# An adaLN block on one core: the second pair's second norm turned by DMA transposes, its first block two blocks later, and POOL or DVE chosen by a changed rule

## The chip, the cores and the metric

The kernel runs on one core of a Trainium2 chip. The metric is the device time of one execution in microseconds. The core's engines work side by side: TensorE (PE) multiplies matrices into PSUM, VectorE (DVE), ScalarE (ACT) and GpSimd (POOL) work on rows, and SyncE (SP) issues the DMAs. Each engine takes its own instructions strictly in the order in which the program gave them to it.

## The reference

A transformer block with adaptive layer norm; x has 2048 rows of 512 values, all in float32.

```python
mod = (_silu(c) @ w_mod).reshape(c.shape[0], 6, 1, -1)      # sa, ca, ga, sb, cb, gb
h = _layernorm(x) * (1 + ca) + sa
x = x + ga * attention(h)      # 32 heads of 128, the last 512 keys and values of the cache, @ wq, @ wo
h = _layernorm(x) * (1 + cb) + sb
x = x + gb * ((gelu(h @ w_gate) * (h @ w_up)) @ w_down)     # inner width 1376
```

## The kernel before

Every matrix product is taken from float16 halves: an operand is a high part and a low part (value minus high part), and a product is three matmuls, high by high, high by low and low by high. The making of these halves is much of what ACT, DVE and POOL do: a scaling of the raw weight, an ACT copy to float16, and a subtraction.

**Attention.** The rows are four groups of 512 (`qg`), two of which make a pair `p`. A slot takes one head and one group, 128 slots in all. It multiplies q by k into `psS` (a pair of PSUM banks, two of them in use), takes the row maxima on DVE (`st<-psS`, two per slot), the exponentials on ACT (`p`, `pp`), the low parts on POOL (`pp<-p,pp`, 128x1024), turns them by DMA transposes (`pT<-pp`), multiplies by v into `psO`, splits the result (`oT`), multiplies by wo into `psW`, and adds into `acc` on DVE. From the third pair of heads on, the q projection of a pair of groups and a pair of heads uses Winograd's form of Strassen's scheme, seven products in place of eight; its sums of weights and activations (`a_sum`, `t_full`, `t_sum`) are elementwise work too.

**The weights' crossings.** `spread_max` (line 667) gets four maxima to all partitions by way of DRAM, reduces them on DVE, turns them into scales `iv` by one tiny `tensor_scalar` on DVE, and takes the reciprocal `av`.

**The second norm and the feed-forward.** `ln_stats` makes mean and reciprocal deviation, `ln2_norm` (line 1363) the normed rows in float32, and `ln2_chunk` (line 1369) turns one of four column chunks by four PE transposes of 128x128 float32 into `psQ`, then applies scale and shift from PSUM. `ln2_high` and `ln2_low` split it. Pair 0 is groups 0 and 1; pair 1, the second pair, groups 2 and 3, made by `chunk2` (line 1817) from the steps in `P1` (line 1843). The inner width is cut into 11 blocks `f` of 128 (the last of 96). A unit `(p, f)` in `UNITS` (line 1764) is one block of one pair; with the same scheme its gate and up products are seven products of six matmuls, 42 matmuls. `aw_make` (line 1822) makes a unit's split weights and their sums; the units left out of `SPLIT` use those that the first pair made for the same block, which in this kernel are blocks 6 to 9 of the second pair.

**What sets the order.** Nothing is issued where the code stands. Every call on an engine is recorded by the `Weaver` with its reads and writes; `issue` (line 412) then plays the whole list several times with a table of costs, forwards and backwards and with random shifts, keeps the order that fares best by that table, and emits it. Some operations are recorded with `either`: the play gives them to one of two engines. `tt` (line 963) does so for POOL and DVE, and carries most subtractions and sums; `affine`, the norms and the scalings do so for other pairs of engines. For operations that hold a resource which POOL and DVE share in the play (the flag `lock`), `sooner` (line 273) adds `SHY`, 1500 ns, to DVE's end when it compares the two. Where POOL's operation is planned close behind such a DVE operation, `issue` makes POOL wait for it. So a change of any step, unit or rule gives a new order on all engines.

Of the kernel before, what the change touches and what calls it, by code (L numbers as in the profile page):

```python
# [10 lines left out]
F32 = mybir.dt.float32  # L11
F16 = mybir.dt.float16
BF16 = mybir.dt.bfloat16
AF = mybir.ActivationFunctionType
OP = mybir.AluOpType
# [3 lines left out]
P = 128  # L19
N = 512  # L20
# [9 lines left out]
NF = (DFF + P - 1) // P  # L30
# [8 lines left out]
HS = 2.0 ** 9  # L39
# [6 lines left out]
ROUND = 1.0 + 2.0 ** -7  # L46
# [43 lines left out]
class Weaver:  # L90
# [159 lines left out]
    def play(self, at, users, span, keep, cut):  # L250
# [6 lines left out]
        free, landed, bus, shared, order = {e: 0.0 for e in self.NEXT}, [], 0.0, {e: 0.0 for e in self.NEXT}, []  # L257
# [15 lines left out]
        def sooner(n, e, t):  # L273

            kinds = self.ops[n][4]
            mine = max(t, shared[e] if kinds[e][1] else 0.0) + kinds[e][0] + (e == "DVE" and kinds[e][1]) * self.SHY
            for o, kind in kinds.items():
                s = max(free[o], ready[n], shared[o] if kind[1] else 0.0)
                if o != e and s + kind[0] + (o == "DVE" and kind[1]) * self.SHY < mine:
                    return max(s, t) + 1.0  # L280
            return None

# [15 lines left out]
        while len(order) < len(self.ops):  # L298
            t, e = min((max(free[e], 0.0 if can[e] else wait[e][0][0]), e) for e in free if can[e] or wait[e])
            while wait[e] and wait[e][0][0] <= t:  # L300
                n = heapq.heappop(wait[e])[1]
# [3 lines left out]
            while can[e] and pick is None:  # L305
                x = heapq.heappop(can[e])
                n = x[1]
# [9 lines left out]
                if e != "SP":  # L317
                    s = pressing(n, e, t, t + self.ops[n][4][e][0] - self.NEXT[e] - 100.0)
# [4 lines left out]
                if len(self.ops[n][4]) > 1:  # L323
                    s = sooner(n, e, t)
# [11 lines left out]
            n = pick  # L336
            by[n] = e
            order.append(n)
            d, lock = self.ops[n][4][e][:2]
# [6 lines left out]
            if lock:  # L346
                t = max(t, shared[e])
# [6 lines left out]
            if e == "SP":  # L354
                if len(landed) >= self.LANES:
                    t = max(t, landed[-self.LANES])
# [95 lines left out]
def adaln_block(ctx: ExitStack, tc: tile.TileContext, x, k_cache, v_cache, wq, wo,  # L452
                w_gate, w_up, w_down, c_in, w_mod, out):
    nc = Weaver(tc.nc, tc)
# [15 lines left out]
    def small(pool, cols_, bufs=3, name="sm"):  # L470
        return pool.tile([P, cols_], F32, name=name, tag=name, bufs=bufs)
# [8 lines left out]
    acc = [rows_[:, t, :] for t in range(SQ // P)]  # L480
    cols = base.tile([P, 16], F32, name="cols")
    colA = {1: cols[:, 0:4], 2: cols[:, 8:12]}
    colB = {1: cols[:, 4:8], 2: cols[:, 12:16]}
# [11 lines left out]
    ffs = base.tile([P, 16], F32, name="ffs")  # L495
# [7 lines left out]
    def b_tile(p, nm, shape=(P, 2, 2, N), dtype=F16):  # L503
        return left1.tile(list(shape), dtype, name=f"{nm}_{p}", tag=f"{nm}_{p}", bufs=1)
# [30 lines left out]

    MV, RS, NMR, LNP, LNF = {}, {}, {}, {}, {}

    def ln_stats(key, src, j):
        if j == 0:
            MV[key] = base.tile([P, 4, 2], F32, name="mv", tag="mv", bufs=4)  # L540
            RS[key] = small(base, 4, 4, "rs")
        st = small(base, 6, 2, "bnst")
        nc.vector.bn_stats(st, src)
        nc.vector.bn_aggr(MV[key][:, j, :], st)
        if j == 3:
            ve = small(base, NC, 2, "ve")
            nc.gpsimd.tensor_tensor(ve, MV[key][:, :, 1], eps_t[:, :NC], op=OP.add)
            nc.gpsimd.tensor_tensor(RS[key], ve, eps_t[:, NC:], op=OP.pow)
            nm = NMR[key] = small(base, 4, 4, "nmr")
            nc.gpsimd.tensor_tensor(nm, MV[key][:, :, 0], RS[key], op=OP.mult)  # L550
            nc.gpsimd.tensor_scalar(nm, nm, -1.0, 1.0, op0=OP.mult, op1=OP.mult)


    def ln_norm(key, dst, src, j, eng=None):
        rs = RS[key][:, j:j + 1]
        if eng is nc.scalar:
            nc.scalar.activation(dst, src, AF.Identity, scale=rs, bias=NMR[key][:, j:j + 1])
        elif eng is nc.gpsimd:
            nc.gpsimd.tensor_scalar(dst, src, MV[key][:, j, 0:1], 1.0, op0=OP.subtract, op1=OP.mult)
            nc.gpsimd.tensor_scalar(dst, dst, rs, 1.0, op0=OP.mult, op1=OP.mult)  # L560
        else:
            nc.vector.tensor_scalar(dst, src, MV[key][:, j, 0:1], rs, op0=OP.subtract, op1=OP.mult)
# [104 lines left out]
    def spread_max(t, top):  # L667
        w = right.tile([P, N], F32, name="sa", tag="sa", bufs=1)
        nc.sync.dma_start(w, t.rearrange("p a -> (p a)").partition_broadcast(P))
        r = small(base, 4, 2, "top")  # L670
        nc.vector.tensor_reduce(r, w.rearrange("p (k a) -> p a k", a=4), op=OP.max, axis=AX.X)
        iv, av = small(base, 8, 5, "iv"), small(base, 8, 5, "av")
        nc.vector.tensor_scalar(iv[:, 0:4], r, 1e-30, ROUND / top, op0=OP.max, op1=OP.mult)
        nc.vector.reciprocal(av[:, 0:4], iv[:, 0:4])
        return iv, av

# [286 lines left out]
    def tt(out_, x_, y_, op, order=(nc.gpsimd, nc.vector)):  # L963
        nc.either(order, lambda o: o.tensor_tensor(out_, x_, y_, op=op))

    def affine(f, pt, a, b):
        nc.either((nc.scalar, nc.vector), lambda o: o.activation(f, pt, AF.Identity, scale=a, bias=b) if o is nc.scalar
                  else o.tensor_scalar(f, pt, a, b, op0=OP.mult, op1=OP.add))
# [226 lines left out]
    s = 36  # L1195
# [73 lines left out]
    def ff_scalars(part):  # L1269
        ab, t = ffs[:, 6:7], ffs[:, 7:8]  # L1270
        if part == 0:
            FS["iv"], av = spread_max(DG.pop("f"), WS)
            nc.vector.tensor_scalar_mul(ffs[:, 0:2], av[:, 0:2], 0.5)
            nc.vector.tensor_scalar_mul(ffs[:, 2:3], av[:, 2:3], 0.5)
            nc.vector.tensor_scalar(ab, FS["iv"][:, 3:4], WS, 1e-25, op0=OP.mult, op1=OP.max)
        iv = FS["iv"]
        if part == 1:
            nc.vector.tensor_scalar(ffs[:, 3:4], ab, iv[:, 0:1], 2.0 / HS, op0=OP.mult, op1=OP.mult)
            nc.vector.tensor_scalar(t, ab, iv[:, 0:1], 2.0, op0=OP.mult, op1=OP.mult)
            nc.vector.tensor_scalar(ffs[:, 5:6], ab, iv[:, 1:2], 4.0 * HID / HS, op0=OP.mult, op1=OP.mult)  # L1280
            nc.vector.tensor_scalar(ffs[:, 5:6], ffs[:, 5:6], iv[:, 2:3], t, op0=OP.mult, op1=OP.mult)
        if part == 2:
            nc.vector.tensor_scalar_mul(t, t, HID)
            nc.vector.reciprocal(ffs[:, 4:5], t)
            nc.vector.reciprocal(ffs[:, 8:9], ab)
            nc.vector.tensor_scalar(cols[:, 8:16], cols[:, 8:16], ffs[:, 8:9], HS, op0=OP.mult, op1=OP.mult)

    s = max(s, 2 * (NIT - 16))
# [49 lines left out]

    N2, FULL, FB, FRAW, AW, WD, WGU, PGU, HID_T, RT, UV, PX = ({} for _ in range(12))
    PLAIN = 2  # L1340
    SLOTS = ("q", "q", "q", "k16", "A1", "A1", "raw2", "raw2")
    SBUFS = {"q": 3, "k16": 1, "A1": 2, "raw2": 2}
    WDTAG = ("kT", "v", "wo", "kT", "kT", "v", "v", "wo", "wo", "oT", "oT")
# [5 lines left out]
    def ff_b(p, nm):  # L1349
        if (p, nm) not in FB:  # L1350
            FB[p, nm] = b_tile(1 - p, nm)
        return FB[p, nm]

    def f_view(qg, c):
        p, r = divmod(qg, 2)
        nm = (("B11", "B21"), ("T4", "B22"))[r][c // 2]
        t = ff_b(p, nm)
        return t[:, 0, c % 2, :], t[:, 1, c % 2, :]

    def ln2_stats(qg, j):  # L1360
        ln_stats(("2", qg), acc[4 * qg + j], j)

    def ln2_norm(qg, j):
        if j % 2 == 0:
# [4 lines left out]
    def ln2_chunk(qg, c, eng=nc.scalar):  # L1369
        key = ("2", qg)  # L1370
        ln_pe(key, [N2[qg, j] for j in range(4)], c, bank("psQ"))
        pt = LNP.pop((key, c))
        if qg == 0:
            full = right.tile([P, N], F32, name="h32", tag="h32", bufs=3)
        else:
            if c % 2 == 0:
                RT["full"] = right.tile([P, 2, N], F32, name="hf", tag="p32", bufs=2)
            full = RT["full"][:, c % 2, :]
        FULL[qg, c] = full
        a, b = colA[2][:, c:c + 1], colB[2][:, c:c + 1]  # L1380
        affine(full, pt, a, b)
# [378 lines left out]
    for c, (a, b, d) in enumerate(((15.5, 15, 16.25), (15, 16.25, 16.5), (16.5, 16, 17.25), (16, 17.25, 17.5))):  # L1760
        at(e + a, ln2_chunk, 0, c)
        at(e + b, ln2_high, 0, c)
        at(e + d, ln2_low, 0, c, nc.gpsimd)
    UNITS = [(0, f) for f in range(PLAIN, 8)] + [(1, 6), (1, 7)] + [(p, f) for f in range(8, NF - 1) for p in range(2)] + \
        [(0, NF - 1)] + [(1, f) for f in range(6)] + [(1, NF - 1)]
    MAKE = {(0, 7): None, (1, 7): 7, (0, 8): 8, (0, 9): 9, (0, 10): 10}
    SPLIT = [u for u in UNITS if not (u[0] and 6 <= u[1] < NF - 1)]
    at(e + 10, aw_load, UNITS[0])
    at(e + 11, aw_load, UNITS[1])
    at(e + 16, aw_scale, UNITS[0])  # L1770
# [44 lines left out]
        f_low(p, c, "T4")  # L1815

    def chunk2(qg, c):
        ln2_chunk(qg, c)
        ln2_high(qg, c)
        ln2_low(qg, c, nc.vector)  # L1820

# [16 lines left out]
    for c in range(2):  # L1838
        sums_b(0, c)
    down_put(0, (0, 1))  # L1840


    P1 = {2: [(ln2_stats, 2, j) for j in range(4)] +
          [(ln2_norm, 2, j) for j in range(4)] + [(chunk2, 2, c) for c in range(4)],
          3: [(ln2_stats, 3, j) for j in range(4)] +
          [(ln2_norm, 3, j) for j in range(4)] + [(chunk2, 3, c) for c in range(4)],
          4: [(sums_a, 1, c) for c in range(2)] + [(sums_b, 1, c) for c in range(2)]}
    WDS = list(range(PLAIN, NF))
    left = {(p, h): 2 if h < NF // 2 else 1 for p in range(2) for h in range(NF // 2 + 1)}
# [75 lines left out]
```

## Time and profile before

| | us |
|---|---|
| median of 3 runs | 1657.41 (1656.83 to 1659.0) |
| the profiled execution's own time | 1657.58 |
| its span, first to last instruction | 1655.8 |
| PE / DVE / ACT / POOL busy | 1642.4 / 1289.3 / 1216.6 / 1305.0 |
| mean granted clock of PE | 0.997 |

How to read it: the span is 1.8 us shorter than the execution's own time, which has what lies around it. A matmul's duration is its time through the pipeline, and consecutive matmuls overlap, so what it costs the stream is the step from one start to the next. A wait of PE counts in full; idle time of the other engines costs nothing unless PE waits for it. All instructions carry line 444, where the `Weaver` emits them, so groups are told apart by the names of their tiles. `h` is a float32 work tile, `hf` another, `B`, `T`, `A`, `S` are split operands of the seven products, `r` and `hid` belong to the feed-forward.

### The profile page before, as it was taken

How to read it: one execution, taken by the hardware profiler on the slowest of the kernel's cores; microseconds unless marked ns; L12 is line 12 of the kernel's file. 1: busy time of each engine (PE TensorE's matmuls, PEld its weight loads, DVE VectorE, ACT ScalarE, POOL GpSimd, SP SyncE). 2: the span in 40 equal slices, each digit the busy share in tenths (PEclk: the TensorE clock that was granted, in tenths of full speed). 3: DMA queues.
4: the chain of work that ended last, by engine and by line, in shares of the span. 5: the costliest groups of instructions: out<-in, count | busy, mean ns of one | idle time of the engine just before them, and what ended most of it. 6: DMA issues, size and time to landing. Idle time of an engine off the chain costs nothing.

```text
span 1655.8 us, 24293 instructions
## 1 busy us (share of the span) xinstructions
PE 1642.4 (99%) x7732; PEld 764.5 (46%) x7732; DVE 1289.3 (78%) x2381; ACT 1216.6 (73%) x2418; POOL 1305.0 (79%) x1097
## 2 busy tenths in 40 slices
PE   8999999999999999999999999999999999999999
PEld 4444444444444444444444444444444444444455
DVE  7777787878787788788999887888887956656557
ACT  5987797777787777888778777787878876545451
POOL 5999986868586878787768889999977898784682
PEclk9999999999999999999999999999999999999999
DMA  7676697878787778999999997788877712101111
GB/s 241 128 144 130 135 157 143 152 138 149 144 143 140 153 136 157 186 196 194 196 200 205 189 167 148 147 175 179 168 129 158 144 28 64 42 25 51 42 45 52
DMA packets 686289, 228.61 MB, mean 138 GB/s; under 512 B 596432, under 2 KB 663056, under 8 KB 686160
## 3 DMA queue, kind: packets, MB, share of 16 engines
q1 hardware_dynamic: 686160, 227.05, 69.1%
q8 instruction: 61, 1.00, 0.3%
q14 instruction: 68, 0.56, 0.1%
HBM read 78.98 MB, written 5.38 MB: 51 GB/s over the span
## 4 chain that ended last, share of the span: by engine, by line
PE 91%; ACT 2%; POOL 2%; DVE 2%; DMA 1%; SPq 1%; issue 1%; DVEq 0%; POOLq 0%; ACTq 0%
PE psS L444 31%; PE psW L444 23%; PE psO L444 21%; PE psQ L444 17%; SPq L444 1%; DVE st L444 1%; DVE acc L444 1%; DMA pT<-pp 1%; ACT p L444 0%; POOL pp L444 0%; POOL B L444 0%; DMA wm<-in_w_mod_dram 0%; POOL aw L444 0%; ACT T L444 0%; DMA raw<-in_B_w_up_dram 0%
## 5 line engine op out<-in xcount | busy, mean ns | idle before, releaser
L444 POOL TENSOR_TENSOR pp<-p,pp 128x1024 f16<-128x1024 f32 x256 | 545.9, 2132 | 212.8 <-ACT pp L444 97.3
L444 ACT ACTIVATE p<-psS,st,es 128x512 f32<-128x512 f32 x512 | 393.4, 774 | 187.7 <-DVE st L444 186.8
L444 DVE SCALAR_TENSOR_TENSOR acc<-psW,st,acc 128x512 f32<-128x512 f32 x496 | 367.2, 742 | 79.8 <-PE psW L444 77.7
L444 PE MATMUL psW<-wo,oT 128*128 128x512 f16 x1536 | 416.3, 379 | 0.0
L444 PE MATMUL psS<-kT,q 128*128 128x512 f16 x1536 | 379.1, 379 | 2.0 <-ACT q L444 2.0
L444 PE MATMUL psO<-pT,v 128*128 128x512 f16 x1536 | 377.1, 379 | 0.3 <-DMA pT<-pp 0.2
L444 DVE TENSOR_REDUCE st<-psS 128x2 f32<-128x1024 f32 x256 | 312.5, 1221 | 60.0 <-PE psS L444 59.6
L444 ACT ACTIVATE pp<-p 128x1024 f16<-128x1024 f32 x256 | 271.0, 1059 | 3.7
L444 PEld LDWEIGHTS <-q 128*128 128x128 f16 x1536 | 149.9, 98 | 182.1 <-ACT q L444 2.6
L444 PEld LDWEIGHTS <-v 128*128 128x128 f16 x1536 | 150.0, 98 | 181.3 <-DMA pT<-pp 1.2
L444 PEld LDWEIGHTS <-oT 128*128 128x128 f16 x1536 | 150.2, 98 | 180.1 <-DVE oT L444 0.5
L444 PEld LDWEIGHTS <-aw 128*128 128x128 f16 (+1 forms) x840 | 84.2, 100 | 95.1 <-issue 2.0
L444 ACT ACTIVATE oT<-psO 128x512 f16<-128x512 f32 x128 | 76.1, 594 | 66.2 <-PE psO L444 66.1
L444 PE MATMUL psQ<-T,S 128*128 128x512 f16 x504 | 123.3, 379 | 0.0
L444 PE MATMUL psQ<-B,A 128*128 128x512 f16 x480 | 119.6, 381 | 0.1
L444 PE MATMUL psS<-T,aw 128*128 128x512 f16 (+1 forms) x480 | 116.9, 379 | 0.0
L444 DVE SCALAR_TENSOR_TENSOR oT<-psO,oT 128x512 f16<-128x512 f32 x128 | 88.0, 688 | 30.9 <-ACT oT L444 30.6
L444 PEld LDWEIGHTS <-A 128*128 128x128 f16 x696 | 68.3, 98 | 83.3 <-issue 2.3
L444 PEld LDWEIGHTS <-S 128*128 128x128 f16 x672 | 65.8, 98 | 79.3
L444 ACT ACTIVATION_READ_ACCUMULATOR p<-psS,st,es 128x1 f32 x512 | 101.0, 197 | 0.0
L444 POOL TENSOR_TENSOR q<-h,q 128x512 f16<-128x512 f32 x84 | 97.5, 1161 | 2.0 <-ACT q L444 1.8
L444 DVE TENSOR_REDUCE mx<-raw 128x1 f32<-128x512 f32 x128 | 84.2, 674 | 15.6 <-DMA raw<-in_A_wq_dram 9.1
(211 smaller groups left out, 2295.6 us busy)
## 6 DMA issues: line engine op xcount, KB each, us to landing
raw<-in_A_k_cache_dram SPq DMA_DIRECT2D x32, 256.0 KB, 3.9
raw<-in_A_wq_dram SPq DMA_DIRECT2D x32, 256.0 KB, 3.7
raw<-in_A_v_cache_dram SPq DMA_DIRECT2D x32, 256.0 KB, 3.3
raw<-in_A_wo_dram SPq DMA_DIRECT2D x32, 256.0 KB, 3.2
pT<-pp SPq DMA_TRANSPOSE x512, 3.3
sa<-most SPq DMA_DIRECT2D x29, 256.0 KB, 3.8
raw<-in_B_w_gate_dram SPq DMA_DIRECT2D x24, 256.0 KB, 3.1
raw<-in_B_w_up_dram SPq DMA_DIRECT2D x24, 256.0 KB, 3.4
```

The lines of the kernel that those rows point to most:

```text
L444: made[n] = real(*a, **k)
```

## The change

Four things change in the code. (1) The second pair's normed rows are scaled (`HS` in `ln_stats`), split into float16 halves, and each half of each row tile is turned by two DMA transposes straight into the tiles in which the products read it; the chunk then applies scale and shift to the turned halves, reading SBUF instead of PSUM, and splits again. (2) `UNITS` puts the second pair's first block after block 9 of the first pair instead of after block 7. Only blocks 8 and 9 of the second pair now share weights with the first pair; blocks 6 and 7 make their own. (3) The tiny scaling in `spread_max` goes to POOL. (4) `SHY` counts only for operations recorded before `nc.calm` is set, which is before the slots of attention are recorded.

```diff
-            mine = max(t, shared[e] if kinds[e][1] else 0.0) + kinds[e][0] + (e == "DVE" and kinds[e][1]) * self.SHY
+            mine = max(t, shared[e] if kinds[e][1] else 0.0) + kinds[e][0] + (e == "DVE" and kinds[e][1]) * (self.SHY if n < self.calm else 0.0)
...
-                if o != e and s + kind[0] + (o == "DVE" and kind[1]) * self.SHY < mine:
+                if o != e and s + kind[0] + (o == "DVE" and kind[1]) * (self.SHY if n < self.calm else 0.0) < mine:
...
+            if big:
+                nc.gpsimd.tensor_scalar(RS[key], RS[key], HS, 1.0, op0=OP.mult, op1=OP.mult)
...
-        nc.vector.tensor_scalar(iv[:, 0:4], r, 1e-30, ROUND / top, op0=OP.max, op1=OP.mult)
+        nc.gpsimd.tensor_scalar(iv[:, 0:4], r, 1e-30, ROUND / top, op0=OP.max, op1=OP.mult)
...
+            nc.vector.tensor_scalar_mul(ffs[:, 9:13], cols[:, 8:12], ffs[:, 8:9])
...
     PLAIN = 2
+    nc.calm = len(nc.ops)
...
+    TURNED = (2, 3)
+
+    def turned_norm(qg, j):
+        if j % 2 == 0:
+            t = b_tile(0, N2TAG[qg][j // 2], (P, 2, 2, 2, N // 2))
+            N2[qg, j], N2[qg, j + 1] = t[:, 0], t[:, 1]
+            RT["norm"] = right.tile([P, 2, N], F32, name="hf", tag="p32", bufs=2)
+        n, t = RT["norm"][:, j % 2, :], N2[qg, j]
+        nc.either((S_, V), lambda o: ln_norm(("2", qg), n, acc[4 * qg + j], j, o))
+        n = n.rearrange("p (a n) -> p a n", a=2)
+        nc.scalar.activation(t[:, :, 0, :], n, AF.Copy)
+        tt(t[:, :, 1, :], n, t[:, :, 0, :], OP.subtract)
+
+    def turned(qg, j):
+        for half in range(2):
+            nm = (("B11", "B21"), ("T4", "B22"))[qg % 2][half]
+            d = ff_b(qg // 2, nm).rearrange("p a c n -> p (a c) n")
+            nc.sync.dma_start_transpose(d[:, :, j * P:(j + 1) * P], N2[qg, j][:, half].rearrange("p a n -> p (a n)"))
+
+    def turned_chunk(qg, c):
+        if c % 2 == 0:
+            RT["full"] = right.tile([P, 2, N], F32, name="hf", tag="p32", bufs=2)
+        full = FULL[qg, c] = RT["full"][:, c % 2, :]
+        a, b = ffs[:, 9 + c:10 + c], colB[2][:, c:c + 1]
+        hi, lo = f_view(qg, c)
+        affine(full, lo, a, b)
+        nc.vector.scalar_tensor_tensor(full, hi, a, full, op0=OP.mult, op1=OP.add)
...
-    UNITS = [(0, f) for f in range(PLAIN, 8)] + [(1, 6), (1, 7)] + [(p, f) for f in range(8, NF - 1) for p in range(2)] + \
-        [(0, NF - 1)] + [(1, f) for f in range(6)] + [(1, NF - 1)]
-    MAKE = {(0, 7): None, (1, 7): 7, (0, 8): 8, (0, 9): 9, (0, 10): 10}
-    SPLIT = [u for u in UNITS if not (u[0] and 6 <= u[1] < NF - 1)]
+    UNITS = [(0, f) for f in range(PLAIN, NF - 1)] + [(1, NF - 3), (1, NF - 2), (0, NF - 1), (1, 6), (1, 7)] + \
+        [(1, f) for f in range(6)] + [(1, NF - 1)]
+    MAKE = {(0, 9): None, (1, 9): 9}
+    SPLIT = [u for u in UNITS if not (u[0] and NF - 3 <= u[1] < NF - 1)]
...
-        ln2_chunk(qg, c)
+        turned_chunk(qg, c)
...
-          [(ln2_norm, 2, j) for j in range(4)] + [(chunk2, 2, c) for c in range(4)],
+          [(g, 2, j) for j in range(4) for g in (turned_norm, turned)] + [(chunk2, 2, c) for c in range(4)],
```

What the new order looks like at two places follows, in rows of the instruction listings. The first is PE in the first pair's third block; `psS_3055` and `psS_3053` are the same product, `T1_0_3045` and `T2_0_3046` hold normed rows of the second pair. Before:

```order
L444 LDWEIGHTS aw_2979
L444 MATMUL psS_3055<-B21_1_2965,aw_2979 128x512
L444 MATMUL psQ_3050<-ident_65,T1_0_3045 128x128 x2
L444 MATMUL psQ_3050<-ident_65,T2_0_3046 128x128 x2
L444 LDWEIGHTS aw_2979
L444 MATMUL psS_3055<-B21_1_2965,aw_2979 128x512
L444 LDWEIGHTS aw_2979
L444 MATMUL psS_3055<-B21_1_2965,aw_2979 128x512
```

And with the change:

```order
L444 LDWEIGHTS aw_2979
L444 MATMUL psS_3053<-B21_1_2965,aw_2979 128x512
L444 LDWEIGHTS aw_2979
L444 MATMUL psS_3053<-B21_1_2965,aw_2979 128x512
L444 LDWEIGHTS aw_2979
L444 MATMUL psS_3053<-B21_1_2965,aw_2979 128x512
```

The four transposes of a chunk, two from each tile of rows, no longer stand between the product's matmuls.

The second place is DVE in early attention, from the 27th row maximum on; `st_479` holds the maxima of one slot, `tf`, `T2_1`, `sa` and `A1` are sums and low parts of the q projection. Before:

```order
L444 TENSOR_REDUCE st_479<-psS_475 128x2
L444 SCALAR_TENSOR_TENSOR acc_72<-psW_477,st_415,acc_72 128x512
L444 TENSOR_SCALAR st_479<-st_479,es_292 128x1 x2
L444 TENSOR_SCALAR iv_387<-top_386 128x4
L444 RECIPROCAL av_388<-iv_387 128x4
L444 TENSOR_SCALAR es_390<-iv_387,sc1_78 128x1
L444 TENSOR_REDUCE st_479<-psS_487 128x2
```

And with the change:

```order
L444 TENSOR_REDUCE st_479<-psS_475 128x2
L444 SCALAR_TENSOR_TENSOR acc_72<-psW_477,st_415,acc_72 128x512
L444 TENSOR_SCALAR st_479<-st_479,es_292 128x1 x2
L444 TENSOR_TENSOR T2_1_94<-tf_410,T2_1_94 128x512
L444 TENSOR_TENSOR tf_444<-tf_444,tf_410 128x512
L444 TENSOR_TENSOR A1_430<-raw_293,A1_430 128x512
L444 TENSOR_TENSOR sa_423<-raw_305 128x256
L444 SCALAR_TENSOR_TENSOR acc_72<-psW_484,st_415,acc_72 128x512
```

Four elementwise operations that POOL did before now stand in DVE's line between a row maximum and the addition that empties the next `psW` bank, and the scaling `iv` is gone from it.

More of the change, by code (lines that the diff above doesn't have):

```diff
@@ L536, in adaln_block, with ln_stats @@
     MV, RS, NMR, LNP, LNF = {}, {}, {}, {}, {}
-    def ln_stats(key, src, j):
+    def ln_stats(key, src, j, big=False):
         if j == 0:
@@ L1360, in ln2_stats @@
     def ln2_stats(qg, j):
-        ln_stats(("2", qg), acc[4 * qg + j], j)
+        ln_stats(("2", qg), acc[4 * qg + j], j, qg in TURNED)
+    TURNED = (2, 3)
[22 more added lines that the diff above has]
+        nc.vector.scalar_tensor_tensor(full, hi, a, full, op0=OP.mult, op1=OP.add)
     def ln2_norm(qg, j):
@@ L1843, in adaln_block @@
     P1 = {2: [(ln2_stats, 2, j) for j in range(4)] +
-          [(ln2_norm, 2, j) for j in range(4)] + [(chunk2, 2, c) for c in range(4)],
+          [(g, 2, j) for j in range(4) for g in (turned_norm, turned)] + [(chunk2, 2, c) for c in range(4)],
           3: [(ln2_stats, 3, j) for j in range(4)] +
-          [(ln2_norm, 3, j) for j in range(4)] + [(chunk2, 3, c) for c in range(4)],
+          [(g, 3, j) for j in range(4) for g in (turned_norm, turned)] + [(chunk2, 3, c) for c in range(4)],
           4: [(sums_a, 1, c) for c in range(2)] + [(sums_b, 1, c) for c in range(2)]}
```

## The prediction

> **What bounds the kernel now.** I read the page's busy times first, then the same by stages, then what TensorE waited for. The first two rows:
>
> ```profile
> span 1655.8 us, 24293 instructions
> ...
> PE 1642.4 (99%) x7732; PEld 764.5 (46%) x7732; DVE 1289.3 (78%) x2381; ACT 1216.6 (73%) x2418; POOL 1305.0 (79%) x1097
> ```
>
> TensorE (PE) is busy throughout, so whatever leaves its stream shortens the run and whatever makes it wait lengthens it. By stages (columns: length, then busy us and instructions of PE, weight loads, DVE, ACT, POOL, then granted clock, DMA share, GB/s):
>
> ```profile
> 0.00:40.00 40.00, 33.54 (x156) 20.08 (x156) 29.06 (x76) 20.76 (x35) 20.25 (x40) 0.91 0.80 250
> 40.00:72.00 32.00, 30.88 (x158) 16.07 (x159) 25.51 (x52) 31.90 (x62) 29.53 (x25) 1.00 0.64 125
> 72.00:202.00 130.00, 130.00 (x605) 58.77 (x603) 95.76 (x185) 104.14 (x211) 126.95 (x96) 1.00 0.72 133
> 202.00:1311.00 1109.00, 1108.73 (x5137) 502.04 (x5135) 921.02 (x1757) 870.23 (x1761) 884.89 (x665) 1.00 0.85 163
> 1311.00:1656.00 345.00, 339.28 (x1682) 167.50 (x1680) 217.99 (x315) 189.58 (x354) 243.40 (x273) 1.00 0.17 48
> ```
>
> The rows are the start, the rest of the filling pipeline, early attention, the rest of attention, and the feed-forward. In early attention POOL is busy 126.95 of 130 us and PE still never idles: a full engine costs nothing while its work can be put off. What PE did wait for, over the whole run (total us, times, longest):
>
> ```profile
> PE psS L444 <- ACT q L444: 2.0, 2, 1.3
> PE psQ L444 <- POOL ident masks.py:199: 1.3, 1, 1.3
> PE psO L444 <- ACT h L444: 1.2, 1, 1.2
> PE psO L444 <- ACT acc L444: 1.1, 3, 0.8
> PE psW L444 <- DVE h L444: 0.7, 2, 0.4
> PE psS L444 <- POOL B L444: 0.6, 1, 0.6
> PE psS L444 <- ACT r L444: 0.5, 1, 0.5
> PE psQ L444 <- POOL A L444: 0.5, 1, 0.5
> PE psS L444 <- DVE r L444: 0.4, 1, 0.4
> PE psS L444 <- DVE sc L444: 0.3, 1, 0.3
> PE psO L444 <- DMA pT<-pp: 0.2, 1, 0.2
> ```
>
> Three of them (POOL B 0.6, ACT r 0.5, DVE r 0.4: 1.5 us) lie in the feed-forward, the pT wait in attention; the other 7.1 us lie in the start. There is little waiting left to remove. What the change can take away is TensorE work; what it can add is waiting.
>
> **The change part by part.** *Transposes.* The second pair's norm now crosses to columns by 16 DMA transposes, so 32 PE transposes go. They are the 32 of this group; a run of four of them, with the matmuls behind it, stands below it:
>
> ```profile
> L444 PE MATMUL psQ<-ident,T 128*128 128x128 f32 x32 | 5.6, 276 | 0.0
> ```
>
> ```profile
> 1365.94 0.60 PE L444 MATMUL psQ<-ident,T 128*128 128x128 f32 x4
> 1366.37 1.24 PE L444 MATMUL psO<-wd,hid 128*128 128x512 f16 x5
> ```
>
> The 276 ns is the time through the pipeline; what counts is the step. Four take 1366.37 - 1365.94 = 0.43 us, 0.1075 each: 32 x 0.1075 = 3.4 us off the PE stream. No other matmul is added or dropped. A page of the Trainium skill gives another figure for this: VectorE: DVE Perf Modes, section The three transpose paths, has 390 ns for a 128x128 transpose on TensorE against 1309 ns by DMA, so by it 32 x 390 ns = 12.5 us would go, an estimate; the trace's step decides, and the term stays 3.4.
>
> *The new path.* Each of 8 row tiles gets one ACT copy, one subtraction and two DMA transposes of 128x512; each of 8 chunks one DVE multiply-add more. The nearest rows:
>
> ```profile
> pT<-pp SPq DMA_TRANSPOSE x512, 3.3
> ```
>
> ```profile
> L444 DVE SCALAR_TENSOR_TENSOR r<-r,ffs 128x512 f32<-128x512 f32 x28 | 25.0, 907 | 0.4
> L444 POOL TENSOR_TENSOR aw<-raw,aw 128x512 f16<-128x512 f32 x14 | 17.2, 1232 | 23.3 <-ACT aw L444 14.9 <-DVE r L444 7.5 <-ACT r L444 0.9
> L444 POOL TENSOR_TENSOR S1f<-raw 128x256 f32<-128x256 f32 x14 | 11.9, 851 | 3.3 <-issue 1.3 <-ACT r L444 1.2 <-POOL aw L444 0.7
> L444 POOL TENSOR_SCALAR raw<-raw,ffs 128x512 f32<-128x512 f32 x6 | 4.2, 698 | 1.1 <-PE psQ L444 1.1
> ```
>
> Latency per tile grows by some 3.3 us of DMA, 1.2 of subtraction and 0.9 of multiply-add. The cover is the first pair's blocks: the second pair's first block comes two blocks later, and a block is 42 matmuls, about 9 us by PE's rate in the table (130 us / 605 = 0.215). If that cover failed, the first second-pair product would wait those 5.4 us. On SP the 16 transposes stand before some w_down loads; the DMA share there is 0.17 of 1.00, so I take 0.
>
> *Two blocks lose shared weights.* Blocks 6 and 7 of the second pair make their own: per block, at most 9 half-size operations at 0.851, one at 1.232 and two scalings at 0.698, 10.3 us on POOL, 21 us for both, plus 4 loads. POOL has 345 - 243.40 = 101.6 us free in this stage and is relieved below: 0.
>
> *The scaling on POOL.* 29 tiny operations leave DVE. Their readers are weights loaded long ahead: 0 either way.
>
> *The penalty.* `SHY` now holds only below `calm`, which is set before the slots are recorded. So nearly all of the program loses DVE's 1500 ns handicap. By the instruction listings DVE gets 201 SBUF-to-SBUF TENSOR_TENSOR in attention where it had one, and 121 in the feed-forward where it had 36. POOL keeps 24 of the large pp in early attention, and its 57 of 512 fall to 19. What such an operation costs on DVE the feed-forward shows (ns min/median/max; then the mean of the 512s):
>
> ```profile
> L444 DVE TENSOR_TENSOR hid<-r,hid x36: 675/692/1534, 1340.6 to 1643.3; 128x512 f16<-128x512 f32 x32, 96x512 f16<-96x512 f32 x4
> ```
>
> ```profile
> L444 DVE TENSOR_TENSOR hid<-r,hid 128x512 f16<-128x512 f32 x32 | 28.3, 897 | 4.3 <-ACT hid L444 4.1
> ```
>
> ```profile
> L444 POOL TENSOR_TENSOR pp<-p,pp 128x1024 f16<-128x1024 f32 x256 | 545.9, 2132 | 212.8 <-ACT pp L444 97.3 <-issue 91.9 <-DVE acc L444 4.5
> L444 POOL TENSOR_TENSOR wo<-raw,wo 128x512 f16<-128x512 f32 x32 | 37.1, 1161 | 0.6 <-ACT wo L444 0.5
> ```
>
> Mostly 692 ns, on POOL 1161; but some took 1534, and the mean is 0.2 above the median. The tightest place is early attention: 43 such operations (five are half-size) enter between the 9th and the 33rd row maximum. In the run before these start here:
>
> ```profile
> 72.73 1.21 DVE L444 TENSOR_REDUCE st<-psS 128x2 f32<-128x1024 f32 x1
> ...
> 201.66 1.22 DVE L444 TENSOR_REDUCE st<-psS 128x2 f32<-128x1024 f32 x1
> ```
>
> At most 43 x 0.692 = 29.7 us, so DVE goes from 95.76 to about 125.5 of 130. At 0.2 extra each (8.6 us) it would be 4 us over. Behind such an operation on DVE stand the row maxima that ACT's exponentials need and the additions that empty psW. Against it stands DVE's lead, as its waits in this stretch show:
>
> ```profile
> DVE acc L444 <- PE psW L444: 13.6, 13, 2.4
> DVE st L444 <- PE psS L444: 9.7, 11, 3.3
> ```
>
> DVE is up to 3.3 us early, so a lag of some us mostly eats its lead, and the later stage has room again (921.02 of 1109). The new waiting of PE lies between 0 and the overfill, some 4 us, or, were stalls longer, 10 (the second rival). I take 0.8, near the lower end, since PE did not wait behind a full POOL either.
>
> *Reordered start.* Its chain is the same; one wait more or less like the longest there (1.3) bounds it: 0, +-1.3. *Feed-forward waits:* 1.5 us now; I keep them.
>
> Sum on the profiled execution: -3.4 + 0.8 = -2.6, span 1653.2. That execution's own time was 1657.58, 0.2 above the median of the runs, so on the median: **1654.8 us**.
>
> **The rivals.** *Waits go as well.* POOL is relieved, and the feed-forward's 1.5 us and one start wait of 1.3 vanish, with no new one: -3.4 - 1.5 - 1.3 = -6.2, 1651.2. For it: one of the three waits is POOL's own. Against: two end on ACT and DVE, which get no lighter.
>
> *DVE blocked by POOL.* In attention POOL's pp holds 2132 ns, longer than any operation beside which hid was seen. If each of the 43 loses half of the longest excess seen, (1534 - 692) / 2 = 421 ns, that is 18.1 us: DVE would want 143.6 of 130, and beyond its lead of 3.3 PE waits 10.3 us. Less 3.4: +6.9, **1664.3, slower**. It ends the gain from a mean of (130 + 3.3 + 3.4 - 125.5) / 43 = 0.26 us, against 0.2 measured. Against it: POOL's work in that stretch falls by 38 x 1.161 = 44 us. A page states the mechanism: the Trainium skill, SBUF — State Buffer, section SBUF: two separate sides, says that a VectorE operation with two SBUF inputs and a GpSimd operation share one port pair as an exclusive lock, whose loser blocks for the whole instruction. The 1534 ns agrees with it; by it alone the worst would be 43 x 2.132 = 92 us, an estimate.
>
> *The change does not do what it says.* The DMA path lands too late after all, and the first second-pair block waits 3 to 5 us: -2.6 + 3 to 5.4 is +0.4 to +2.8, 1657.8 to 1660.2. Against it: two more blocks of cover, 18 us.
>
> **How the numbers follow.** 0.2% (3.3 us) is about what a measurement of this kernel can tell from no change: 1654.1 to 1660.7. My forecast, 0.55, has its own range of 1652.9 to 1657.4 (waits gone or 3.4 of new ones); about a third of it lies below 1654.1. Waits go: 0.20. DVE blocked: 0.17. Path late: 0.08. So faster 0.18 + 0.20 = 0.38, same 0.37 + 0.08 = 0.45, slower 0.17. The range runs from the first rival's 1651.2 into the second's, to 1662.0, leaving out about 0.14.
>
> **What would show it.** Right: 7700 matmuls; none from ident in the feed-forward's second pair; SBUF operations on DVE in attention near 692 ns median; DVE near 125 and POOL near 85 of the 130 us; PE waits below 2 us between 60 and 1311 us. Wrong: waits `psS <- ACT p`, `psW <- DVE acc` or `psO <- DMA pT` of several us in early attention (second rival); a wait on B, T or hf tiles before the second pair's first block (third).

## The result, and the profile after

The changed kernel takes 1662.84 us (median; 1658.77 to 1669.02), the kernel before 1657.47 beside it: a ratio of 1.0035 [1.0029, 1.0041], so 5.4 us slower. It also varies more from run to run, by 10.3 us where before varies by 3.8. The profiled execution is one of the faster ones, 1659.68 us, 3.2 below its median. Its page begins:

```profile
span 1657.9 us, 24455 instructions
...
PE 1638.5 (99%) x7700; PEld 760.4 (46%) x7700; DVE 1457.2 (88%) x2651; ACT 1224.9 (74%) x2431; POOL 1046.7 (63%) x877
```

The 32 transposes are gone from PE, and about 168 us of work has gone onto DVE. By stages, in the columns of before:

```profile
0.00:40.00 40.00, 32.23 (x164) 20.37 (x165) 31.71 (x83) 24.12 (x41) 19.72 (x41) 0.96 0.84 250
40.00:72.00 32.00, 31.25 (x162) 16.42 (x161) 29.64 (x60) 29.43 (x60) 25.55 (x18) 1.00 0.79 144
72.00:202.00 130.00, 129.15 (x599) 58.14 (x597) 123.89 (x236) 103.81 (x209) 85.29 (x61) 1.00 0.74 136
202.00:1311.00 1109.00, 1104.64 (x5108) 499.43 (x5107) 996.66 (x1861) 861.11 (x1733) 731.23 (x533) 1.00 0.84 161
1311.00:1658.00 347.00, 341.22 (x1673) 166.08 (x1671) 275.26 (x415) 206.47 (x391) 184.96 (x227) 1.00 0.23 60
```

Busy time hides the loss; the number of matmuls shows it. Between 202 and 1311 us PE did 5108 where before did 5137. A kernel below does 5141 there without one wait, 0.2157 us each, so the 29 are 6.3 us; the six fewer between 72 and 202 us are 1.3. The start, before and then after, up to 72 us:

```profile
0.00:72.00 72.00, 64.42 (x314) 36.14 (x315) 54.56 (x127) 52.65 (x96) 49.78 (x65) 0.95 0.73 195
```

```profile
0.00:72.00 72.00, 63.48 (x324) 36.79 (x325) 61.35 (x142) 53.55 (x100) 45.27 (x59) 0.98 0.82 203
```

Here the changed kernel is ten matmuls ahead (some 2.2 us, though not all are of one size there). So 6.3 + 1.3 - 2.2 - 3.4 (the transposes) = +2.0, against a span longer by 2.1. The remaining 3.2 us to the median lie in executions that left no trace.

What PE waited for from 202 to 1311 us, and then the largest of DVE's waits for DMAs in the same stretch:

```profile
PE psW L444 <- DVE acc L444: 3.5, 6, 1.8
PE psQ L444 <- ACT h L444: 0.4, 1, 0.4
```

```profile
DVE top L444 <- DMA sa<-most: 12.7, 10, 2.0
```

Before, PE waited 0.2 us in all of 72 to 1311, and DVE 7.2 for these loads. `sa<-most` is the crossing's load: four maxima come back from DRAM on all partitions, and `top` reduces them on DVE. The place with PE's longest wait, on SP, on DVE and on PE (start, length, and in brackets the idle time before it):

```profile
846.77 0.52 SPq L444 DMA_DIRECT2D sa<-most  x1
```

```profile
849.19 0.33 DVE L444 TENSOR_SCALAR st<-st,es 128x1 f32<-128x1 f32 x2
851.49 1.11 DVE L444 TENSOR_REDUCE top<-sa 128x4 f32<-128x512 f32 x1 [1.98 <-DMA sa<-most]
853.30 0.52 DVE L444 TENSOR_REDUCE mff<-raw 128x1 f32<-128x352 f32 x1 [0.71 <-DMA raw<-in_B_w_up_dram]
853.74 0.74 DVE L444 SCALAR_TENSOR_TENSOR acc<-psW,st,acc 128x512 f32<-128x512 f32 x1
```

```profile
852.37 0.38 PE L444 MATMUL psW<-wo,oT 128*128 128x512 f16 x1
854.53 0.38 PE L444 MATMUL psW<-wo,oT 128*128 128x512 f16 x1 [1.79 <-DVE acc L444]
```

The crossing's load is issued at 846.77 and read at 851.49. Behind it in DVE's line stands `mff`, which reads a weight that is loaded from DRAM too, and behind that the addition that empties psW. While the loads fly, DVE does nothing, and PE stands still behind it for 1.79 us. Both loads are late, but the wait that ends last here is that of the weight's load, and the chain of what ended last runs through it:

```profile
848.35 4.93 DMA raw<-in_B_w_up_dram
```

With the crossing's load in time alone, `mff` would have started no sooner, as its weight landed at 853.28. At another place nothing but the crossing's load is late. DVE, then PE:

```profile
415.23 1.09 DVE L444 TENSOR_REDUCE top<-sa 128x4 f32<-128x512 f32 x1 [0.78 <-DMA sa<-most]
416.23 0.74 DVE L444 SCALAR_TENSOR_TENSOR acc<-psW,st,acc 128x512 f32<-128x512 f32 x1
416.88 0.69 DVE L444 SCALAR_TENSOR_TENSOR oT<-psO,oT 128x512 f16<-128x512 f32 x1
417.48 0.75 DVE L444 SCALAR_TENSOR_TENSOR acc<-psW,st,acc 128x512 f32<-128x512 f32 x1
```

```profile
418.28 0.38 PE L444 MATMUL psW<-wo,oT 128*128 128x512 f16 x1 [0.45 <-DVE acc L444]
```

Followed back in this way, the matmuls between 202 and 1311 us that start over 0.1 us later than the usual step lose 6.7 us together: 3.7 in nine places behind crossing loads, 2.0 in the one place behind the weight's load, the rest behind other things. In before they lose 0.6 us in two places, neither behind a crossing load. The chain of what ended last has these crossing loads on it (start, us):

```profile
181.37 4.48 DMA sa<-most
...
207.89 4.62 DMA sa<-most
...
411.72 3.48 DMA sa<-most
...
813.21 3.82 DMA sa<-most
...
976.75 3.99 DMA sa<-most
...
1137.75 3.85 DMA sa<-most
```

There are six. In the chain of before no such load is among the longest pieces.

### The profile page after: what moved, and what is told of

The parts are those of the page before. It is cut to its first block, busy times and chain, and to the rows that moved or that the text cites. A ratio compares the mean times of both kernels' runs of the same rounds, so it can differ in the third digit from the quotient of the medians.

```text
span 1657.9 us, 24455 instructions
## 1 busy us (share of the span) xinstructions
PE 1638.5 (99%) x7700; PEld 760.4 (46%) x7700; DVE 1457.2 (88%) x2651; ACT 1224.9 (74%) x2431; POOL 1046.7 (63%) x877
## 4 chain that ended last, share of the span: by engine, by line
PE 85%; DVE 7%; DMA 3%; ACT 2%; SPq 1%; issue 1%; POOL 0%; ACTq 0%; POOLq 0%; DVEq 0%
PE psS L444 29%; PE psW L444 21%; PE psO L444 19%; PE psQ L444 15%; DVE st L444 2%; DVE acc L444 1%; DMA sa<-most 1%; SPq L444 1%; ACT p L444 1%; DVE h L444 1%; DVE mx L444 1%; DVE top L444 0%; DVE q L444 0%; DVE bnst L444 0%; DVE oT L444 0%
## 5 line engine op out<-in xcount | busy, mean ns | idle before, releaser
L444 PE MATMUL psW<-wo,oT 128*128 128x512 f16 x1536 | 469.9, 379 | 3.9 <-DVE acc L444 3.5
L444 PE MATMUL psO<-pT,v 128*128 128x512 f16 x1536 | 426.1, 379 | 0.0
L444 PE MATMUL psS<-kT,q 128*128 128x512 f16 x1536 | 423.4, 379 | 1.6 <-ACT q L444 0.9
L444 PE MATMUL psQ<-T,S 128*128 128x512 f16 x504 | 142.3, 379 | 0.4 <-ACT h L444 0.4
L444 PE MATMUL psQ<-B,A 128*128 128x512 f16 x480 | 132.7, 379 | 0.6 <-DVE q L444 0.4
L444 DVE SCALAR_TENSOR_TENSOR oT<-psO,oT 128x512 f16<-128x512 f32 x128 | 87.7, 685 | 11.3 <-ACT oT L444 9.7
L444 PE MATMUL psS<-B,aw 128*128 128x512 f16 (+1 forms) x360 | 88.6, 379 | 0.0
```

The costliest lines, as they stand in the source:

```text
L444: made[n] = real(*a, **k)
```

## The experiments

The first theory, from this trace: **late loads** on DVE's line, which DVE, now nearly full, is too little ahead of PE to absorb. The expectations call it theory lead. Its rivals: the **port** (the prediction's second rival; theory lock), the **parts** (the turned norm, the later block or the new order costs the time), and the **draw** (the planner gives each altered program another order, and before's is a fortunate one; against it stands theory change, that the loss is the change's own in any order). All runs are in this table; columns: time, ratio to before on the same chip, then of the profiled execution the matmuls and DVE's busy time between 202 and 1311 us, DVE's wait for `sa<-most` over the whole span, and the number of these loads among the longest pieces of the chain.

| run | us | ratio | PE x | DVE us | wait | chain |
|---|---|---|---|---|---|---|
| before | 1657.47 | | 5137 | 921 | 7.2 | 0 |
| changed | 1662.84 | 1.0035 [1.0029, 1.0041] | 5108 | 997 | 13.8 | 6 |
| penalty_kept | 1669.81 | 1.0078 [1.0065, 1.0091] | 5102 | 910 | 17.4 | 5 |
| penalty_lifted_only | 1669.20 | 1.0074 [1.0061, 1.0087] | 5083 | 991 | 15.0 | 7 |
| lifted_in_ffn_only | 1653.97 | 0.9981 [0.9972, 0.9990] | 5125 | 917 | 8.4 | 1 |
| lifted_in_ffn_only_draw_5 | 1662.77 | 1.0033 [1.0021, 1.0046] | 5095 | 910 | 22.7 | 6 |
| before_late_landing | 1660.86 | 1.0024 [1.0015, 1.0033] | 5132 | 924 | 0 | 0 |
| changed_late_landing | 1658.22 | 1.0006 [0.9997, 1.0015] | 5126 | 999 | 0 | 0 |
| penalty_kept_late_landing | 1663.78 | 1.0043 [1.0029, 1.0057] | 5141 | 921 | 0 | 0 |
| penalty_lifted_late_landing | 1660.62 | 1.0023 [1.0013, 1.0032] | 5141 | 999 | 0 | 0 |
| before_other_draw | 1661.04 | 1.0020 [1.0011, 1.0029] | 5132 | 921 | 10.5 | 2 |
| before_draw_3 | 1660.76 | 1.0022 [1.0013, 1.0031] | 5123 | 922 | 17.5 | 5 |
| before_draw_5 | 1657.41 | 1.0004 [0.9995, 1.0013] | 5130 | 922 | 11.3 | 2 |
| changed_other_draw | 1662.39 | 1.0034 [1.0022, 1.0046] | 5102 | 999 | 14.7 | 8 |
| changed_draw_3 | 1655.27 | 0.9987 [0.9978, 0.9996] | 5125 | 996 | 17.4 | 4 |
| changed_draw_5 | 1671.96 | 1.0088 [1.0074, 1.0102] | 5076 | 980 | 17.1 | 7 |
| before_pp_halves | 1663.39 | 1.0031 [1.0020, 1.0042] | 5122 | 920 | 12.8 | 2 |
| changed_pp_halves | 1653.53 | 0.9980 [0.9971, 0.9989] | 5140 | 1004 | 5.2 | 1 |
| changed_pp_across | 1659.28 | 1.0005 [0.9996, 1.0014] | 5128 | 996 | 6.7 | 2 |
| changed_pp_halves_late | 1655.46 | 0.9987 [0.9979, 0.9996] | 5134 | 1013 | 0 | 0 |

The last four columns are of one execution each, which can lie up to 3.6 us from its median (before_draw_5: 1660.98). Before itself took 1656.52 to 1657.59 us on the chips of the experiments, so a difference between two rows of different chips is uncertain by about 1 us. The chain of lifted_in_ffn_only can be followed back only to 1135.8 us, so its 1 counts that part alone.

### The penalty taken apart from the rest

Changed kernel, penalty everywhere (both lines of `sooner` alike):

```diff
-... (e == "DVE" and kinds[e][1]) * (self.SHY if n < self.calm else 0.0)
+... (e == "DVE" and kinds[e][1]) * self.SHY
```

> The changed kernel with DVE's 1500 ns penalty left on everywhere, so only the turned norm, the later block and the scaling on POOL remain. Theory lead (DVE's moved work uses up its lead over TensorE, and its waits for DMAs then reach TensorE): faster than before, 1652 to 1656 us, PE waits on psW from DVE's additions under 1 us. Theory lock (DVE blocked by POOL at the shared resource): the same figures. Rival parts (the turned norm, the later block or the new draw of the order costs the time): 1660 us or more.

The kernel before with the reverse edit and `nc.calm = len(nc.ops)` ahead of the slots:

> The kernel before with the penalty lifted after the prologue and nothing else changed. Theories lead and lock: the whole loss and more, since the 3.4 us of transposes stay: 1662 to 1668 us. Rival parts: within 3 us of before.

Each half alone costs more than the whole: +13.3 us and +12.7 us beside 1656.52. Theories lead and lock expected 1652 to 1656 for the first, and 1662 to 1668 for the second; the rival parts had the first right (1660 or more), but the second within 3 us of before. None of them has both. The trace of the first shows two losses. In attention there are late loads again. In the feed-forward, between 1440 and 1500 us (columns of the stages; before, then penalty_kept, then the changed kernel):

```profile
1440.00:1500.00 60.00, 59.03 (x273) 26.50 (x271) 37.71 (x50) 31.32 (x59) 45.14 (x49) 1.00 0.13 35
```

```profile
1440.00:1500.00 60.00, 54.52 (x246) 23.62 (x245) 40.19 (x52) 37.18 (x65) 48.74 (x48) 1.00 0.28 64
```

```profile
1440.00:1500.00 60.00, 58.85 (x271) 26.27 (x270) 56.45 (x86) 38.23 (x68) 17.24 (x20) 1.00 0.18 45
```

27 matmuls fewer than before, 5.8 us, with POOL at 48.74 of 60; in the changed kernel POOL falls to 17.24 there and only two are missing. The largest of PE's waits at that place (1430 to 1520) end on several engines:

```profile
PE psS L444 <- DVE r L444: 1.8, 2, 1.4
PE psS L444 <- ACT h L444: 1.5, 2, 0.8
PE psO L444 <- ACT hid L444: 1.0, 1, 1.0
PE psS L444 <- POOL T L444: 1.0, 1, 1.0
```

So the turned norm and the own weights of two more blocks seem to need DVE's help in the feed-forward; which of the two does, no run shows. Later I lifted the penalty there alone, first with the seed of the change, then with 5:

```diff
-    nc.calm = len(nc.ops)
     SLOTS = ("q", "q", "q", "k16", "A1", "A1", "raw2", "raw2")
...
         slot(i)
+    nc.calm = len(nc.ops)
```

> The changed kernel, with the penalty lifted from the start of the feed-forward slots on alone, so that in attention the two-input operations stay on POOL as before. Theory lead: DVE's idle time in attention comes back, PE's waits on psW behind DVE go to under 1 us, and the time is 1652 to 1658. Rival (the loss is made elsewhere, by the later weights or the turned norm, and the spread by the draw of any order): 1660 to 1670.

> The same kernel with the planner's draws seeded with 5, the seed with which the changed kernel took 1671.96 us. Theory lead: with DVE's lead back, the draw matters little, and it comes within 3 us of the run with seed 7. Rival: the seed costs 5 us or more here too.

The first expectation of theory lead held in its time (1653.97), though PE waited 1.4 us on psW where it had under 1; the second did not hold: seed 5 costs 8.8 us here too. Between 1440 and 1500 us PE does 272 matmuls in both, so lifting the penalty there is enough for the feed-forward. And at both seeds the kernel is faster than the changed one with the same seed, by 8.9 us (seed 7) and 9.2 us (seed 5). With seed 5 DVE has its idle time back, 910 of 1109 us busy, and PE waits all the same on DVE (202 to 1311 us), as some loads come up to 5.3 us after DVE is ready for them:

```profile
PE psQ L444 <- DVE q L444: 4.5, 3, 1.6
PE psQ L444 <- DVE h L444: 2.0, 1, 2.0
PE psW L444 <- DVE acc L444: 1.6, 3, 0.7
```

```profile
DVE top L444 <- DMA sa<-most: 22.7, 13, 5.3
```

### Loads planned to land later

In `play`, whoever reads a tile that was loaded out of DRAM scratch is planned 3 us later. Nothing that is computed changes, but the order is drawn anew:

```diff
-... else end + 1500.0 * (m in self.landing))
+... else end + 1500.0 * (m in self.landing) + 3000.0 * (n in self.landing))
```

> The changed kernel with 3 us more counted by the planner between the issue of a load from the DRAM scratch tiles and its reader, so that DVE's reductions of the crossings stand later in its line; the same work, penalty lifted. Theory lead: DVE's wait for these loads (12.7 us in the stretch 202 to 1311 us of the changed kernel) falls under 4 us, the PE waits at these places go, and the time falls by 2 us or more, to 1657 to 1661. Theory lock: no change, 1661 to 1665.

> The kernel before, with 3 us more planned between the issue of a load out of a DRAM scratch tile and its use. It is the control for the changed kernel with the same edit, which fell from 1662.84 to 1658.22 us. Theory lead (in the changed kernel DVE has too little lead over PE to ride out the late crossing loads that stand in its line): before has that lead, waits 7.2 us for these loads without PE waiting behind them, and comes within 1 us of 1657.5. Rival (the crossing loads are planned too early in every order, and the lead has nothing to do with it): it gains as the changed kernel did, 3 to 5 us, to 1653 to 1654.5.

> The changed kernel with the penalty kept everywhere (1669.81 us without it), and 3 us more planned for loads out of DRAM scratch tiles. If what it lost is the same late crossing loads (16.8 us of waits on DVE for them), it falls by 5 us or more, to 1665 or less, and the waits of some 10 us between 1440 and 1520 go with them. If those waits come from POOL, which is busy 48.7 of 60 us between 1440 and 1500 there, it stays at 1664 to 1669, and they stand where they stood.

> The kernel before with the penalty lifted as in the change (1669.2 us without this edit), and 3 us more planned for loads out of DRAM scratch tiles. Theory lead: the lifted penalty costs time only through those loads, so most of the 11.7 us goes, and it comes to 1656 to 1661. Rival lock (POOL keeps DVE off the shared port in the moved operations): the moved operations are still on DVE, so it stays at 1666 to 1669.

Theory lead's times held for the changed kernel (1657 to 1661) and for the lifted penalty (1656 to 1661), where theory lock had 1661 to 1665 and 1666 to 1669. In all four DVE's wait for `sa<-most` is gone, no such load is on the chain, and PE does 5126 to 5141 matmuls between 202 and 1311 us. Each is a new draw too; but all five programs with the edit are free of this wait, and all fifteen without it have 5.2 us or more. In the changed kernel 18 of the 33 matmuls that are missing against 5141 come back; before, which lost little behind these loads, does five fewer than without the edit. The sharpest is the kernel before with the penalty lifted, without the edit and with it:

```profile
202.00:1311.00 1109.00, 1100.84 (x5083) 497.49 (x5082) 991.28 (x1872) 857.55 (x1723) 723.61 (x502) 1.00 0.83 159
```

```profile
202.00:1311.00 1109.00, 1109.00 (x5141) 503.04 (x5140) 999.14 (x1899) 863.12 (x1743) 724.32 (x505) 1.00 0.85 161
```

DVE is as full as before and does all the moved operations beside POOL, yet no wait of PE is listed there. So in this execution neither a full DVE nor the port costs PE anything between 202 and 1311 us once the loads are there in time; 58 matmuls, 12.5 us, came back.

The times fell less than that, because the feed-forward was redrawn as well. penalty_kept_late_landing came to 1663.78, under the 1665 of its first expectation, but still loses in the feed-forward (PE x229 between 1440 and 1500), as its second had it, and before_late_landing, 3.9 us slower than before in spite of its clear attention, met neither expectation.

### Other draws of the order

The planner's random shifts come from `random.Random(7)`; the edit is the 7.

> The changed kernel with another seed for the planner's random shifts, so with another order of the same kind. Theories lead and lock: 1660 to 1667 us again, with waits on psW from DVE's additions at other places. If the loss came of one unlucky draw: within 3 us of 1654.8.

> The kernel before, with the planner's random draws seeded with 11 in place of 7, as was done with the changed kernel (1662.39 against 1662.84 us). Theory change (the loss of 5.4 us is the change's own, whatever order is drawn): it stays within 1.5 us of 1657.5. Rival draw (before's order is a fortunate one of many that the planner could draw, and any new costs redraw it): it comes out at 1660 to 1664, 3 to 6 us slower with no change made.

> The kernel before with the planner's draws seeded with 3. Theory draw: before's own order is a fortunate one, so this comes out at 1659 to 1664, as seed 11 did (1661.04). Theory change: before's orders lie at 1656 to 1659 and seed 11 was the odd one.

> The changed kernel with the planner's draws seeded with 3. Theory draw: it lies anywhere in 1655 to 1664, and the mean of its four seeds comes within 2.5 us of before's four. Theory change: it lies at 1661 to 1664 like seeds 7 and 11, with before's mean 4 us or more below.

> The kernel before with the planner's draws seeded with 5. Theory draw: 1659 to 1664. Theory change: 1656 to 1659.

> The changed kernel with the planner's draws seeded with 5. Theory draw: anywhere in 1655 to 1664. Theory change: 1661 to 1664.

Before's four draws: 1657.5, 1661.0, 1660.8, 1657.4, mean 1659.2. The changed kernel's: 1662.8, 1662.4, 1655.3, 1672.0, mean 1663.1. The means differ by 3.9 us, between the bounds that I had set (2.5 and 4); taken against before on the same chip it is 4.2, and a spread of 16.7 us makes such a mean worth little. Theory change missed before's seeds 11 and 3 and the changed kernel's seeds 3 and 5; theory draw missed seed 5 of both kernels. The changed kernel's seed 11 met theories lead and lock (1660 to 1667). One thing stands: at seed 3 the changed kernel is the faster by 5.5 us. PE's waits behind DVE from 202 to 1311 us, at seed 3 and at seed 5:

```profile
PE psW L444 <- DVE acc L444: 1.1, 3, 0.5
```

```profile
PE psW L444 <- DVE acc L444: 6.4, 9, 1.8
```

DVE waits as long for the loads in both (17.4 and 17.1 us over the whole span). What the one order does to absorb it and the other does not, I did not find out.

### POOL's hold of the port

`s_low`'s subtraction (2.13 us on POOL) in two halves; in the other form the halves run across, so that both transposes still wait for both.

```diff
-        nc.gpsimd.tensor_tensor(pp[:, :, 1, :], p32, pp[:, :, 0, :], op=OP.subtract)
+        for j in range(2):
+            nc.gpsimd.tensor_tensor(pp[:, j, 1, :], p32[:, j, :], pp[:, j, 0, :], op=OP.subtract)
```

> The changed kernel with the POOL subtraction of the probabilities' low part issued in two halves of 512 columns, so that POOL's longest hold of the shared port in attention is halved; no other operation is altered. Rival lock: the mean stall of DVE's two-input operations halves, and the time falls by 2 us or more, to 1661 or less. Theory lead: the loss is not the port, and it stays within 1.5 us of 1662.8, or is longer by what 80 more POOL instructions cost.

> The kernel before, with POOL's subtraction of the probabilities' low part in two halves of 512 columns, the control for the changed kernel with the same edit (which fell from 1662.84 to 1653.53 us). Before has almost no two-input operation on DVE between tiles in SBUF during attention. If the edit helps by giving DVE the shared port sooner, nothing is gained here: 1656 to 1659. If it helps because the first of the two transposes that follow goes out 1 us earlier, or by a better order in any kernel, it gains here too: 1654 or less.

> The changed kernel with that subtraction in two halves across (columns 0 to 255 of both 512s, then 256 to 511), so that POOL's hold of the port is halved as in the other form, but both transposes still wait for both halves. If the gain of 9.3 us came from the port, it comes here too: 1652 to 1656. If it came from the earlier first transpose, it is gone: 1661 to 1665.

> The changed kernel with the halves of 512 columns (1653.53 us alone) and 3 us more planned for loads out of DRAM scratch tiles (1658.22 us alone). If the two cure the same waits, it comes out at 1652 to 1655; if they cure different ones, at 1647 to 1650. A time above 1656 would say that the order drawn weighs more than either edit.

The first result, 9.3 us better, looked like the port. The others do not bear it out: the same halving across gives 3.6, between its two expectations, the kernel before loses 5.9 by the edit, which neither account had, and the late landing on top takes 1.9 away again (1655.46, between its expectations for the same waits, up to 1655, and for the draw, above 1656). Nor did the operations get as much shorter as they would have. The subtractions for q and v on DVE between 202 and 1311 us, changed kernel, then with halves:

```profile
L444 DVE TENSOR_TENSOR q<-h,q 128x512 f16<-128x512 f32 x46 | 35.2, 764 | 0.8 <-ACT q L444 0.7
L444 DVE TENSOR_TENSOR v<-raw,v 128x512 f16<-128x512 f32 x21 | 20.8, 991 | 0.0
```

```profile
L444 DVE TENSOR_TENSOR q<-h,q 128x512 f16<-128x512 f32 x53 | 39.1, 739 | 0.2 <-ACT q L444 0.2
L444 DVE TENSOR_TENSOR v<-raw,v 128x512 f16<-128x512 f32 x19 | 15.9, 838 | 0.0
```

They are shorter by 25 and 153 ns, 1.2 and 2.9 us over all of them, but those for k and wo are longer (738 to 892 ns and 723 to 758). Over all TENSOR_TENSOR of more than 0.6 us in this stretch the mean falls from 808 to 769 ns, 4.7 us of DVE's time. The stalls over 681 ns make 14.4 us there in the changed kernel, so half of them would be 7.2; the 9.3 us of PE's time are not there. The edit also turns POOL's 256 subtractions into 512; they are 256 more, not the 80 of the expectation. The halves are also an order in which few loads are late (5.2 us, one on the chain). It is the fastest kernel of the study, 1653.53 us, 0.9980 [0.9971, 0.9989] of before, with lifted_in_ffn_only at 1653.97 next to it.

### What they say together

Sorted by the last column of the table, the eight executions with four loads or more on the chain did 5102 matmuls between 202 and 1311 us on average (5076 to 5125), the twelve with two or fewer 5132 (5122 to 5141): 30 matmuls, 6.5 us. So the loss in attention goes with late loads on the chain, whether the penalty is lifted or kept; at the border the two groups meet (both kernels with seed 3 have four or five loads and a small loss). The count is no proof by itself, since the chain goes through a load only where it held something up; the late landings are the test. Followed back as above, crossing loads make 6.0 of the 8.3 us of late starts in penalty_kept, 8.2 of 12.1 in penalty_lifted_only and 6.9 of 13.6 in changed_draw_5. And the change beside before under the same edit, each against before on its own chip, gives +5.4 (as it is), +2.4, -5.5 and +14.6 (seeds 11, 3 and 5), -2.2 (late landing) and -9.3 us (halves). Its sign is not a property of its four parts.

## Why the prediction was wrong

The range ended at 1662.0, 0.8 us under the median, and the sign was wrong.

- **Transposes, -3.4:** right as far as the trace goes. 7700 matmuls, none of `psQ<-ident,T`. The best orders of the changed kernel, 1653.5 to 1655.3, are 2.2 to 3.9 us faster than before; that the transposes give it is not shown.
- **The new path, 0:** right. The 16 transposes land in 2.4 to 2.5 us where I had taken 3.3, and no wait of PE for turned tiles is above 0.2 us, so the third rival did not happen:

```profile
B<-T SPq DMA_TRANSPOSE x12, 2.5
T<-T SPq DMA_TRANSPOSE x4, 2.4
```

- **Two blocks' own weights, 0:** right only beside the lifted penalty. I had set 21 us against POOL's 101.6 free in the whole stage; with the penalty kept, the 60 us from 1440 on lose 5.8 us, with POOL busy 48.74 of them. The average hid the place; whether these weights or the turned norm fill it is open.
- **The scaling on POOL, 0:** DVE's `av` waits 1.9 us in six places for it between 202 and 1311; no run took this part alone.
- **The penalty, +0.8: this is the step that failed**, in its size, its place and its reason. The engines' busy times were right, to 2 us: DVE 123.89 of 130 in early attention (forecast 125.5), POOL 85.29 (85). But PE waited about 1.3 us more there and 6.3 us more between 202 and 1311, where I had written that "the later stage has room again (921.02 of 1109)": at 997 of 1109 it has less. So the term was 7.6 us in place of 0.8, and PE's listed waits from 60 to 1311 us are 4.8, where I had set 2 as the sign of being right. "PE did not wait behind a full POOL either" was the wrong comparison. What PE waits behind here is not how busy an engine is but its order: an instruction at the head of DVE's line whose data is not there yet, most often a crossing's load. The row that says so was in the trace of before (7.2 us, longest 2.2), and I did not read it.
- **The second rival, 1664.3,** came near the time, but its mechanism has not the size for it. The Trainium skill, SBUF — State Buffer, section SBUF: two separate sides, has the loser of the port block for the whole instruction. The trace agrees: between 202 and 1311 us the 45 TENSOR_TENSOR of more than 0.6 us that began while a POOL instruction ran took 1.00 us on average, the 69 others 0.68. In early attention, where the rival had 18.1 us of stalls, the 14 of 41 that began beside POOL took 0.84 on average against 0.68, 2.2 us in all, and PE's listed waits there are 0.9 us, none on psW. And with the moved operations in place no wait of PE is listed between 202 and 1311 us in penalty_lifted_late_landing. That the rival's time came so near is luck.
- **Start, 0 +-1.3:** some 2.2 us gained, a little outside. **Feed-forward waits, 1.5:** PE's listed waits there are 1.8.
- **No term at all** stood for the redrawn order. Before's own four draws differ by 3.6 us, more than the whole forecast gain of 2.6, and the changed kernel's by 16.7.

What is shown: most of the time lost in attention is lost behind loads that land after DVE has come to them, crossing loads above all, and in the three kernels with such a loss where it was tried, all of it (penalty_kept, penalty_lifted_only) or about half (changed) comes back when the crossing loads are planned later. Not settled is whether the lifted penalty puts them there or the redraw alone: 8.9 and 9.2 us at two seeds speak for the penalty, the late loads of penalty_kept and of before_draw_3, where nothing is lifted, for the redraw. Lifting in the feed-forward alone together with the late landing was not tried.

## What to carry to other kernels

Where a planner sets the order, an edit of a cost is a new draw: run a few seeds of both kernels before you believe a difference of a few us, and give the forecast a term for it. Read for each engine which instructions of its line wait for a DMA and how long, since an engine with idle time can absorb this, and a full one hands more of it on; in lifted_in_ffn_only_draw_5 idle time was not enough. To find which of two waits in a row counts, take the one that ends last. Look at the load of the narrowest 60 us, not of the stage.

## What the hardware showed that I had not expected

A wait of PE can be paid twice. In penalty_kept DVE waits 3.08 us for a crossing load up to 789.76 us, and PE then stands still behind DVE for 2.08 us, up to 794.45 us. Columns as in the stages; the granted clock is the third value from the end:

```profile
786.00:792.00 6.00, 6.00 (x30) 2.70 (x29) 2.89 (x4) 2.17 (x4) 3.83 (x4) 1.00 1.11 239
792.00:796.00 4.00, 1.92 (x9) 0.74 (x8) 3.29 (x8) 3.68 (x8) 2.11 (x4) 0.94 1.06 281
796.00:799.00 3.00, 3.00 (x9) 1.11 (x8) 1.32 (x4) 3.00 (x8) 3.00 (x2) 0.52 0.87 153
799.00:805.00 6.00, 6.00 (x30) 2.70 (x29) 4.39 (x8) 5.63 (x14) 5.65 (x6) 1.00 0.91 174
```

After the wait the clock is granted at 0.52 for 3 us: 9 matmuls start where 14 would at full clock, about 1.1 us more in that window. After the changed kernel's wait of 1.79 us, from 854 us on, the clock stays at 1.00, and so it does after one of 2.05 us up to 771.12 us in lifted_in_ffn_only_draw_5. The Trainium skill, TensorE: Matmul & The Clock Gate, section Part 1: The HAM clock gate (the "warmup" mystery), has the clock halved after an idle window of about 3.4 us, in windows that run free of the program; the half rate agrees, while the wait ahead of it here was only 2.08 us. What sets apart the 2.08 from the 2.05 us, no run here shows.
